# Splitting and joining both 16-bit planes of a DMA transposition in one instruction, for 8 of 24 rows of tokens

## The chip, the cores and the metric

The kernel runs on one core of a Trainium2 chip. The core has five engines that run their own instruction streams in order and wait for each other by semaphores: PE (TensorE, matrix products, writes PSUM), DVE (VectorE), ACT (ScalarE), POOL (GpSimd) and SP (SyncE, which here only issues DMAs). The metric is the device time of one execution in microseconds, as the median of several runs.

## The reference

Chunked attention with memory keys, followed by a two-layer network with a softmax-weighted, normalised hidden layer (cut to the core):

```python
# attention: 4 batches, 8 heads, 768 positions, head_dim 64; chunks of 32 queries
scores = scale * q_c @ k_full.T            # k_full: 8 memory keys + 56 keys of context
a = exp(scores - max(scores)); a = a / (sum(a) + 1e-9)
out_c = a @ v_full
x = out.transpose(0, 2, 1, 3).reshape(3072, 512)
# network, per row of x
h = x @ w_in                               # 512 -> 1024
e = exp(h - max(h)); sm = e / (sum(e) + 1e-9)
solu = h * sm
ln = (solu - mean(solu)) / sqrt(var(solu) + 1e-6) * g_ln
return ln @ w_out                          # 1024 -> 512
```

## The kernel before

The 3072 tokens are 24 **rows of tokens** t of 128 each, and 12 pairs u of such rows (t = 2u and 2u + 1). All work is cut into steps, and the string ORDER at the top of the file lists every step in the order in which it is written to the engines; no scheduler moves anything. A name such as `Us6.1@G` is the step Us of row 6, part 1, on POOL (`@S` ACT, `@G` POOL, `@V` DVE). Since each engine runs in order, the place of a name in ORDER decides what stands in front of an instruction on its engine.

The steps of the attention go by pairs: loads of k, q and v on SP (Lk, Lq, Lv), scores on PE (S), row maximum and its subtraction on DVE (M, Bm), exponentials on ACT (X), row sums on DVE (Z), the transposed probabilities (p), values on PE (V), normalisation on DVE (N), and the transposed result (x). The rounded high part XH of x and the remainder XL (x minus XH, on DVE at L215) are what G reads: `hidden` (L482), four blocks of six matmuls G t.0 to G t.3 for each row, of which the third matmul of a block is the first one that reads XL.

The steps of the network go by rows: G, row maximum Hm (DVE L491), exponential He (ACT L496), product and sum Hu (DVE L506, L509), square Sq (ACT L514), subtraction of the mean C (DVE L524), four small instructions Dn for the scale (POOL L530 to L533), the transposition of u, its high part UH and remainder UL, and O: `project` (PE L543), eight blocks of three matmuls O t.0 to O t.7; then scaling Os and the store St from ACT.

A transposition of a 128x1024 float32 tile (p, x or u) goes through DMA, which transposes 16-bit elements only. Two split instructions copy the lower and the upper halves of all words into two planes of 1024 16-bit elements (Ps, Xs, Us; part 0 and part 1). One DMA transposition issued from SP (Px, Xx, Ux; L338) moves both planes. Two join instructions interleave the planes again (Pm, Xm, Um). A split or a join is one copy of 128x1024 16-bit elements, on ACT (L210) or on POOL (L212); ORDER says which. All tiles of this path lie in 12 buffers "slot" of SBUF, taken and given back in a ring.

The PSUM buffers "two" (three of them) hold, in turn, the scores of a pair, the values of a pair and the hidden row h. A new holder waits until the last reader of the one before is done: h is free after Sq, scores after Bm, values after N.

```python
def halves(ap):
    return ap.bitcast(U16).rearrange("p (n two) -> p two n", two=2)
def planes(ap):
    return ap.bitcast(U16).rearrange("p (two n) -> p two n", two=2)
```

Of the kernel before, what the change touches and what calls it, by code (L numbers as in the profile page):

```python
# [33 lines left out]
W7@S R8 D14 G0.3 D15 W8@S G1.3 Hm0 A10 G2.3 B10 He0 Hm1 R9 A11 E10 H10@S Hu0 He1 B11 T10 H11@S E11
R10 Sq0 Hu1 W9@S G3.0 Dn0@G T11 A12 C0 Sq1 R11 B12 Hm2 A13 Dn1@G G3.1 H12@S E12 B13 A14 UT0 T12
H13@S E13 G3.2 UH0@S B14 T13 A15 G3.3 E14 H14@S C1 W10@S B15 T14 W11@S R12 H15@S E15 UL0@V He2 R13
T15 W12@S UT1 Hu2 W13@S R14 UH1@S Hm3 Sq2 R15 UL1@V W14@S Dn2@G W15@S C2 O0.0 He3 S2 Hu3 O0.1 Lk4
Lq4 O1.0 O0.2 M2 Sq3 O1.1 O0.3 C3 Dn3@G S3 Bm2 O0.4 Lk5 Lq5 M3 X2 O1.2 O0.5 Ps2.0@G O1.3 Z2 S4
Ps2.1@G Bm3 O0.6 Px2 Lk6 Lq6 UT2 M4 X3 O0.7 UH2@S O1.4 Ps3.0@G Z3 UT3 Os0 Ps3.1@G O1.5 Bm4 UH3@S St0
Px3 O1.6 Pm2.0@G UL2@V X4 O1.7 Pm2.1@G Os1 UL3@V S5 Ps4.0@S St1 Z4 V2 Ps4.1@G O2.0 Pm3.0@S Lv4 N2  # L40
Px4 O3.0 O2.1 M5 Pm3.1@G Xs2.0@S O3.1 O2.2 Xs2.1@G Bm5 V3 Xx2 O2.3 X5 N3 Lv5 Pm4.0@G O3.2 Ps5.0@S
O2.4 Z5 Xs3.0@G O3.3 Pm4.1@S O2.5 Ps5.1@G O3.4 Xs3.1@G Px5 V4 Xm2.0@S Xx3 O2.6 N4 Xm2.1@G O3.5 O2.7
Xs4.0@S XH2@G O3.6 S6 Os2 Xs4.1@G XL2@V Pm5.0@S St2 Lv6 O3.7 Xx4 Os3 Pm5.1@G M6 Lk7 Lq7 G4.0 Xm3.0@S
St3 G5.0 Bm6 Xm3.1@G G4.1 X6 XH3@G G5.1 Xm4.0@S Ps6.0@G Z6 G4.2 Ps6.1@G Xm4.1@S XL3@V Px6 G5.2 XH4@G
G4.3 XL4@V G5.3 Hm4 G6.0 Pm6.0@G Hm5 He4 G6.1 Pm6.1@G He5 Hu4 G6.2 Hu5 Sq4 G6.3 Sq5 C4 Dn4@G G7.0
Hm6 Us4.0@S Dn5@G G8.0 C5 He6 Us4.1@G G7.1 Us5.0@S Hu6 Ux4 G8.1 Us5.1@G Sq6 G7.2 Ux5 G8.2 C6 Dn6@G
Lk8 Lq8 Us6.0@S G7.3 Um4.0@G Us6.1@S V5 Hm7 Um4.1@G Ux6 G8.3 Um5.0@S N5 Lv7 UH4@G He7 Hm8 G9.0
Xs5.0@G Um5.1@G UL4@V Xs5.1@S G9.1 He8 UH5@G Xx5 G9.2 Hu7 Um6.0@S O4.0 G9.3 UL5@V Sq7 Um6.1@G O4.1
Hu8 O5.0 Xm5.0@S O4.2 Dn7@G C7 O5.1 UH6@S Hm9 O4.3 Xm5.1@G Us7.0@S O5.2 UL6@V O4.4 XH5@G Sq8 O5.3
O4.5 Us7.1@S C8 O5.4 Dn8@G O4.6 He9 Ux7 XL5@V O5.5 Us8.0@G O4.7 Hu9 G10.0 Os4 Us8.1@G St4 Sq9 O5.6  # L50
V6 Ux8 C9 Dn9@G Um7.0@S O5.7 Lv8 N6 G10.1 Us9.0@G Os5 Xs6.0@S St5 S7 Um7.1@G Us9.1@S Xs6.1@G O6.0 M7
Lk9 Lq9 G10.2 UH7@S Ux9 Um8.0@G Xx6 Bm7 O6.1 Um8.1@G G10.3 UL7@V X7 UH8@G O6.2 Ps7.0@S G11.0 Hm10
Ps7.1@S O6.3 Um9.0@G Z7 O7.0 He10 Px7 O6.4 Um9.1@G UL8@V G11.1 Xm6.0@S O6.5 Xm6.1@G Hu10 O7.1 O6.6
G11.2 Pm7.0@G Sq10 O6.7 Pm7.1@G C10 O7.2 Os6 G11.3 XH6@G UH9@S St6 Us10.0@S O7.3 Hm11 Dn10@G V7
Us10.1@S XL6@V O7.4 He11 Ux10 O8.0 N7 O7.5 G12.0 UL9@V Xs7.0@G O7.6 Lv9 Hu11 G12.1 Xs7.1@G Sq11 O7.7
Um10.0@G Xx7 G12.2 Os7 C11 Dn11@G Um10.1@S St7 S8 Us11.0@G UH10@S O8.1 M8 Lk10 Lq10 G12.3 Us11.1@G
UL10@V Xm7.0@S O8.2 Ux11 G13.0 Bm8 Xm7.1@G O8.3 Hm12 O9.0 X8 O8.4 Ps8.0@G Z8 G13.1 He12 Um11.0@G
O8.5 Ps8.1@S Hu12 O9.1 Um11.1@G Px8 O8.6 Sq12 G13.2 C12 Dn12@G O8.7 O9.2 Os8 G13.3 XH7@G Us12.0@S
St8 UH11@G O9.3 Pm8.0@S XL7@V S9 Us12.1@G Pm8.1@S O9.4 Hm13 Lk11 Lq11 G14.0 Ux12 M9 He13 O9.5 G14.1
UL11@V O9.6 Bm9 O10.0 O9.7 Hu13 X9 Um12.0@G V8 Os9 Z9 Ps9.0@G G14.2 Lv10 Sq13 St9 Um12.1@G N8 O10.1  # L60
Ps9.1@S G14.3 Dn13@G C13 UH12@S Px9 O10.2 Hm14 Xs8.0@G Us13.0@S G15.0 UL12@V Xs8.1@G He14 O10.3
O11.0 Us13.1@S Hu14 O10.4 Xx8 G15.1 Pm9.0@G Ux13 Sq14 O10.5 Pm9.1@G O11.1 C14 O10.6 Dn14@G G15.2
Us14.0@S Xm8.0@G O10.7 Us14.1@S O11.2 Xm8.1@G G15.3 Os10 Ux14 Um13.0@S St10 O11.3 XH8@G Hm15 V9
Um13.1@S XL8@V O11.4 Lv11 He15 UH13@G O12.0 N9 O11.5 Um14.0@S G16.0 UL13@V Xs9.0@G Um14.1@S O11.6
Hu15 G16.1 Xs9.1@G Sq15 O11.7 Xx9 G16.2 UH14@G Os11 C15 Dn15@G St11 S10 UL14@V Us15.0@S O12.1 M10
G16.3 Us15.1@G Xm9.0@G Ux15 Bm10 O12.2 G17.0 Xm9.1@G Hm16 X10 O12.3 Ps10.0@G Z10 O13.0 He16 O12.4
Ps10.1@G G17.1 Hu16 Um15.0@S Px10 O12.5 Sq16 O13.1 Um15.1@G O12.6 G17.2 C16 Dn16@G Us16.0@S S11
Us16.1@G Pm10.0@S O12.7 M11 O13.2 Ux16 XH9@G Os12 G17.3 Pm10.1@S UH15@G Bm11 St12 O13.3 XL9@V X11
V10 Hm17 Ps11.0@G O13.4 G18.0 Um16.0@S Ps11.1@G N10 O13.5 He17 Um16.1@G Px11 UL15@V G18.1 Xs10.0@S
O13.6 O14.0 Xs10.1@G Hu17 O13.7 G18.2 Xx10 Os13 UH16@G Z11 Sq17 St13 Pm11.0@G O14.1 UL16@V G18.3  # L70
Dn17@G Pm11.1@S O14.2 C17 G19.0 Hm18 Us17.0@G Xm10.0@S O14.3 Us17.1@G He18 V11 Xm10.1@G Ux17 O14.4
N11 O15.0 O14.5 Hu18 Xs11.0@G G19.1 Xs11.1@G Sq18 O14.6 O15.1 Xx11 Um17.0@G C18 O14.7 G19.2 Os14
XH10@G Um17.1@S St14 O15.2 Us18.0@G G19.3 XL10@V Dn18@G Us18.1@S O15.3 O16.0 Xm11.0@S Hm19 UH17@G
Ux18 O15.4 G20.0 UL17@V He19 Xm11.1@G O15.5 Hu19 G20.1 O15.6 Sq19 Um18.0@G O16.1 O15.7 C19 Dn19@G
Um18.1@S G20.2 XH11@G Os15 O16.2 Us19.0@S G20.3 St15 UH18@G Us19.1@G G21.0 Hm20 Ux19 O16.3 He20
G21.1 Hu20 O16.4 G21.2 Sq20 O16.5 Um19.0@G O17.0 C20 O16.6 Dn20@G Um19.1@S G21.3 Us20.0@G O16.7
XL11@V UH19@S O17.1 Us20.1@G Os16 O17.2 Hm21 St16 G22.0 Ux20 UL18@V He21 O17.3 G22.1 UL19@V O17.4
Hu21 G22.2 Sq21 O17.5 Um20.0@G G22.3 C21 Dn21@G Um20.1@S O17.6 Hm22 O18.0 Us21.0@G O17.7 He22 O18.1
UH20@G G23.0 Os17 Us21.1@G Hu22 St17 O18.2 Ux21 G23.1 UL20@V Sq22 O18.3 C22 Dn22@G O19.0 Us22.0@S
O18.4 G23.2 Us22.1@G Um21.0@S O18.5 Ux22 O19.1 Um21.1@G O18.6 G23.3 O18.7 Hm23 UH21@G O19.2 Os18  # L80
UL21@V O19.3 He23 Um22.0@G St18 O20.0 O19.4 Hu23 O20.1 O19.5 Um22.1@G Sq23 O20.2 O19.6 UH22@G C23
O20.3 Dn23@G O19.7 UL22@V O20.4 Os19 UT23 St19 O21.0 UH23@S O20.5 O21.1 UL23@V O20.6 O21.2 O20.7
O21.3 Os20 O21.4 St20 O22.0 O21.5 O22.1 O21.6 O22.2 O21.7 O22.3 Os21 O22.4 St21 O23.0 O22.5 O23.1
O22.6 O23.2 O22.7 O23.3 Os22 O23.4 St22 O23.5 O23.6 O23.7 Os23 St23
"""


# [554 lines left out]
```

## Time and profile before

| what | value |
|---|---|
| median of 3 runs | 381.53 us |
| the runs | 376.96, 381.53, 382.13 us |
| the profiled execution: span from its first to its last instruction | 379.2 us (its own time is not listed beside it; the span lies 2.3 us below the median of the runs) |
| PE busy | 354.1 us (93%) |
| DVE, ACT, POOL busy | 220.7, 199.4, 199.5 us (58%, 53%, 53%) |
| mean granted clock of PE | 0.972 |
| DMA transpositions | 39, median 5.2 us from issue to landing |

A row of a timeline has the start in us, the duration in us, engine, line, operation, the tiles written and read with shapes, the number of instructions merged, and in brackets the idle time of the engine ahead of it and what ended that. A row of a group has the count, the busy time, the mean duration in ns, and the idle time ahead of the group with its releasers.

### The profile page before, as it was taken

The numbers are of one execution on the slowest core, as the hardware profiler recorded it, in microseconds if no ns is written. First come the engines' busy times: TensorE is split into PE (matmuls) and PEld (weight loads), VectorE is DVE, ScalarE is ACT, GpSimd is POOL, SyncE is SP. The second block draws the span as 40 slices with busy tenths as digits, with TensorE's granted clock in tenths as the row PEclk, the third lists the DMA queues.
The fourth block names the chain that finished last, engine by engine and source line by source line (L and its number), as shares of the span: only waits on it lengthen the run. The fifth ranks groups of instructions, "written<-read, shape, count | busy, mean of one in ns | idle before, by whom it ended". The sixth has DMA issues, their size and how long they took to land.

```text
span 379.2 us, 10107 instructions
## 1 busy us (share of the span) xinstructions
PE 354.1 (93%) x4408; PEld 279.3 (74%) x4408; DVE 220.7 (58%) x287; ACT 199.4 (53%) x259; POOL 199.5 (53%) x236
## 2 busy tenths in 40 slices
...
GB/s 277 399 404 404 251 114 3 0 143 291 135 259 188 236 162 62 217 183 131 309 159 195 218 114 213 199 201 161 111 127 99 140 56 85 84 74 93 28 55 55
DMA packets 96859, 62.90 MB, mean 166 GB/s; under 512 B 82480, under 2 KB 82480, under 8 KB 96816
## 3 DMA queue, kind: packets, MB, share of 16 engines
...
HBM read 35.52 MB, written 6.29 MB: 110 GB/s over the span
## 4 chain that ended last, share of the span: by engine, by line
PE 69%; DMA 11%; POOL 6%; issue 5%; ACT 5%; DVE 3%; POOLq 0%; ACTq 0%
PE one L543 28%; PE two L482 24%; DMA slot<-slot 11%; PE two L434 4%; POOL slot L212 4%; PE two L372 3%; PE one L286 3%; PE two L357 3%; PE two L199 2%; DVE fr L215 1%; ACT two L514 1%; ACT slot L210 1%; ACT fr L210 1%; PE one L288 1%; PE one L287 1%
## 5 line engine op out<-in xcount | busy, mean ns | idle before, releaser
L212 POOL TENSOR_SCALAR slot<-slot 128x1024 uint16<-128x1024 uint16 x94 | 119.6, 1296 | 61.3 <-DMA slot<-slot 34.1
L482 PE MATMUL two<-w_in_h,fr 128*128 128x512 f32 x384 | 134.0, 401 | 6.9 <-ACT two L514 3.7
L543 PE MATMUL one<-w_out_h,fr 128*128 128x512 f32 x384 | 135.9, 404 | 0.1
L210 ACT COPY slot<-slot 128x1024 uint16<-128x1024 uint16 x62 | 73.3, 1206 | 45.0 <-DMA slot<-slot 30.8
L482 PEld LDWEIGHTS two<-w_in_h,fr 128*128 128x128 f32 x384 | 72.9, 190 | 24.3 <-ACT two L514 4.4
L543 PEld LDWEIGHTS one<-w_out_h,fr 128*128 128x128 f32 x384 | 73.1, 190 | 20.1 <-issue 1.8
L543 PE MATMUL one<-w_out_l,fr 128*128 128x512 f32 x192 | 76.4, 398 | 1.5 <-issue 1.5
L482 PE MATMUL two<-w_in_l,fr 128*128 128x512 f32 x192 | 76.4, 398 | 0.0
L215 DVE TENSOR_TENSOR fr<-slot,fr 128x1024 fp32r<-128x1024 f32 x29 | 43.3, 1497 | 23.1 <-POOL fr L212 18.7
L491 DVE TENSOR_REDUCE per_row<-two 128x1 f32<-128x1024 f32 x24 | 29.1, 1218 | 28.2 <-PE two L482 28.1
L482 PEld LDWEIGHTS two<-w_in_l,fr 128*128 128x128 f32 x192 | 36.6, 191 | 10.1 <-issue 1.9
L543 PEld LDWEIGHTS one<-w_out_l,fr 128*128 128x128 f32 x192 | 36.6, 191 | 7.7
L514 ACT ACTIVATE two<-slot,per_row 128x1024 f32<-128x1024 f32 x24 | 26.8, 1117 | 23.5 <-DVE per_row L509 23.5
L496 ACT ACTIVATE slot<-two,per_row 128x1024 f32<-128x1024 f32 x24 | 26.8, 1116 | 18.0 <-DVE per_row L491 17.1
L212 POOL TENSOR_SCALAR fr<-slot 128x1024 fp32r<-128x1024 f32 x23 | 25.6, 1119 | 18.7 <-ACT slot L210 9.2
L524 DVE TENSOR_SCALAR slot<-slot,per_row 128x1024 f32<-128x1024 f32 x24 | 22.1, 922 | 21.8 <-ACT two L514 21.6
L551 ACT ACTIVATE o_sb<-one,per_row 128x512 f32<-128x512 f32 x24 | 16.4, 684 | 34.5 <-PE one L543 34.5
L506 DVE CUSTOM_DVE_ANT_0 slot<-two,slot 128x1024 f32<-128x1024 f32 x24 | 29.1, 1213 | 5.8 <-ACT slot L496 5.8
L530 POOL TENSOR_SCALAR per_row<-per_row 128x1 f32<-128x1 f32 x24 | 10.9, 453 | 33.0 <-ACT slot L496 31.3
L409 ACT ACTIVATE slot<-slot 128x1024 f32<-128x1024 f32 x12 | 12.7, 1061 | 29.1 <-DVE slot L401 29.1
L446 DVE TENSOR_TENSOR slot<-two,per_head 128x1024 f32<-128x1024 f32 x12 | 14.6, 1217 | 21.7 <-PE two L434 15.0
L434 PE MATMUL two<-v,slot 64*32 64x64 f32 x1536 | 19.6, 239 | 7.1 <-issue 5.5
...
## 6 DMA issues: line engine op xcount, KB each, us to landing
...
slot<-in_w_in SPq DMA_DIRECT2D x8, 512.0 KB, 12.0
...
slot<-slot SPq DMA_TRANSPOSE x39, 5.2
g_col<-in_g_ln SPq DMA_DIRECT2D x1, 4.0 KB, 12.3
```

Of the source, the lines that this page charges most:

```text
L210: nc.scalar.copy(out, in_)
L212: nc.gpsimd.tensor_scalar(out, in_, 1.0, 0.0, ALU.mult, ALU.add)
L215: (nc.gpsimd if on == "G" else nc.vector).tensor_tensor(out, a, b, ALU.subtract)
L434: nc.tensor.matmul(x[32 * j:32 * j + 32, r, t, g], pT[rows, t, g, 32 * j:32 * j + 32], vv[rows, t, g, j], start=True, stop=True,)
L482: nc.tensor.matmul(h[:, half], x[a], w[b][:, c, half * HALF:(half + 1) * HALF], start=c == 0 and i == 0, stop=c == NC_ - 1 and i == 2,)
L491: nc.vector.tensor_reduce(take("per_row", ("hm", t), 1), flat(get("h", t)), axis=AX.X, op=ALU.max, negate=True)
L496: nc.scalar.activation(take("slot", ("u", t), 3), flat(get("h", t)), AF.Exp, bias=get("hm", t), scale=1.0, accum_out=take("per_row", ("esu ...
L506: nc.vector.tensor_tensor_reduce(u, flat(get("h", t)), u, 1.0, 0.0, ALU.mult, ALU.add, accum_out=usum)
L514: nc.scalar.activation(flat(get("h", t)), get("u", t), AF.Square, bias=get("nmu", t), scale=1.0, accum_out=take("per_row", ("var", t), 1),)
L524: nc.vector.tensor_scalar(u, u, get("nmu", t), None, ALU.add)
L543: nc.tensor.matmul(get("o", t), u[a], w[b][:, f], start=f == 0 and i == 0, stop=f == NF - 1 and i == 2)
L551: nc.scalar.mul(take("o_sb", ("osb", t), 1), get("o", t), get("rstd", t))
```

## The change

For rows 6, 7, 8, 9 and 12, 13, 14, 15 of tokens the two splits Us become one instruction and the two joins Um become one instruction, each of 2 x 1024 16-bit elements. The instruction stands in ORDER where the second part stood. The engines are DVE for rows 6, 9, 12 and 15, ACT for rows 7 and 13, POOL for rows 8 and 14; split and join of a row are on one engine. Rows 6, 7, 8 and 12 walk plane by plane (Usb, Umb: first all lower halves, then all upper ones). Rows 9, 13, 14 and 15 walk element by element (Use, Ume: lower and upper half of a word, then the next word). So 32 copies of 1024 elements go (18 on ACT, 14 on POOL), and 16 of 2048 elements come (8 on DVE, 4 on ACT, 4 on POOL). The DMA transpositions and their places on SP stay.

```diff
+    def split_both(name, elements):
+        def step(i, on):
+            s = planes(take("slot", (name + "s", i), 1))
+            x = halves(get(name, i))
+            if elements:
+                s, x = (ap.rearrange("p two n -> p n two") for ap in (s, x))
+            copy(on, s, x)
+            used(name, i)
+            used(name, i)
+        return step
+
+    def join_both(name, uses, elements):
+        def step(i, on):
+            out = halves(take("slot", (name + "T", i), uses))
+            x = planes(get(name + "t", i))
+            if elements:
+                out, x = (ap.rearrange("p two n -> p n two") for ap in (out, x))
+            copy(on, out, x)
+            used(name + "t", i)
+            used(name + "t", i)
+        return step
...
-        UT=on_pe("u"), Us=split("u", 2), Ux=xbar("u"), Um=join("u", 2), UH=high("u", 1), UL=low("u", 1),
+        UT=on_pe("u"), Us=split("u", 2), Ux=xbar("u"), Um=join("u", 2),
+        Usb=split_both("u", False), Use=split_both("u", True),
+        Umb=join_both("u", 2, False), Ume=join_both("u", 2, True), UH=high("u", 1), UL=low("u", 1),
```

In ORDER, for example, `Us12.0@S ... Us12.1@G` becomes `Usb12@V`, and `Us14.0@S Xm8.0@G O10.7 Us14.1@S O11.2 Xm8.1@G` becomes `Xm8.0@G O10.7 Use14@G O11.2 Xm8.1@G`.

Three places show what that does to the streams. The first is DVE around the split of row 12. Before, behind the remainder of pair 7 (fr_74, XL7) stand the row maximum of h13, a memset and the row maximum of the scores of pair 9 (M9), the remainder UL11, and Bm9:

```order
L215 TENSOR_TENSOR fr_74<-slot_65,fr_75 128x1024
L491 TENSOR_REDUCE per_row_114<-two_82 128x1
L389 MEMSET two_83 32x2x4x16
L393 TENSOR_REDUCE per_head_99<-two_83 128x16
L215 TENSOR_TENSOR fr_80<-slot_68,fr_73 128x1024
L401 TENSOR_TENSOR slot_71<-two_83,per_head_99 128x2x8x64
```

Now (line numbers of the changed file; L207 is the copy on DVE) the split of row 12 is in between:

```order
L214 TENSOR_TENSOR fr_74<-slot_63,fr_75 128x1024
L207 COPY slot_69<-slot_72 128x2048
L512 TENSOR_REDUCE per_row_114<-two_82 128x1
L410 MEMSET two_83 32x2x4x16
L414 TENSOR_REDUCE per_head_99<-two_83 128x16
L214 TENSOR_TENSOR fr_80<-slot_68,fr_73 128x1024
L422 TENSOR_TENSOR slot_66<-two_83,per_head_99 128x2x8x64
```

Everything from the row maximum of h13 to Bm9 has moved behind one more copy.

The second place is POOL around the split of row 14. Before, behind the joins Pm9 come the four instructions of Dn14, both joins Xm8 and the high part XH8 (fr_77), then UH13 (fr_75):

```order
L212 TENSOR_SCALAR slot_72<-slot_65 128x1024 x2
L530 TENSOR_SCALAR per_row_109<-per_row_109 128x1
L531 TENSOR_SCALAR per_row_109<-per_row_109 128x1
L532 TENSOR_SCALAR per_row_109<-per_row_104,per_row_109 128x1
L533 TENSOR_TENSOR per_row_123<-per_row_109,mhalf 128x1
L212 TENSOR_SCALAR slot_66<-slot_68 128x1024 x2
L212 TENSOR_SCALAR fr_77<-slot_66 128x1024
L212 TENSOR_SCALAR fr_75<-slot_64 128x1024
```

Now the split of row 14 (128x1024x2), which was on ACT, stands between the two joins Xm8:

```order
L211 TENSOR_SCALAR slot_71<-slot_63 128x1024 x2
L551 TENSOR_SCALAR per_row_109<-per_row_109 128x1
L552 TENSOR_SCALAR per_row_109<-per_row_109 128x1
L553 TENSOR_SCALAR per_row_109<-per_row_104,per_row_109 128x1
L554 TENSOR_TENSOR per_row_123<-per_row_109,mhalf 128x1
L211 TENSOR_SCALAR slot_66<-slot_68 128x1024
L211 TENSOR_SCALAR slot_65<-slot_62 128x1024x2
L211 TENSOR_SCALAR slot_66<-slot_68 128x1024
L211 TENSOR_SCALAR fr_77<-slot_66 128x1024
L211 TENSOR_SCALAR fr_75<-slot_64 128x1024
```

XH8 has moved behind that copy, and so has what reads it.

The third place is ACT around the split of row 13. Before, the two parts stand on both sides of the exponential He14 (L496), and Sq14 (L514) and the two parts of row 14 follow:

```order
L210 CAST fr_76<-slot_69 128x1024
L210 COPY slot_62<-slot_63 128x1024
L496 ACTIVATE slot_61,per_row_109<-two_81,per_row_117 128x1024
L210 COPY slot_62<-slot_63 128x1024
L514 ACTIVATE two_81,per_row_104<-slot_61,per_row_100 128x1024
L210 COPY slot_71<-slot_61 128x1024 x2
```

Now one instruction stands between He14 and Sq14, and those of row 14 are gone:

```order
L209 CAST fr_76<-slot_70 128x1024
L517 ACTIVATE slot_62,per_row_109<-two_81,per_row_117 128x1024
L209 COPY slot_69<-slot_67 128x1024x2
L535 ACTIVATE two_81,per_row_104<-slot_62,per_row_100 128x1024
```

More of the change, by code (lines that the diff above doesn't have):

```diff
@@ L34 @@
[L34 to L84, printed above, removed]
+V0 T0 H0@S B1 A3 R0 Lv2 N0 H1@S W0@S E1 XT0 B3 A2 T1 H3@S B2 R1 XH0@S E3 E2 H2@S T3 W1@S XL0@V R3
```

57 lines of the change are left out of this document (53 added, 4 removed).

## The prediction

> **What bounds the kernel now.** I read the busy times first, then a table by stage, then what PE waits for.
>
> ```profile
> span 379.2 us, 10107 instructions
> PE 354.1 (93%) x4408; PEld 279.3 (74%) x4408; DVE 220.7 (58%) x287; ACT 199.4 (53%) x259; POOL 199.5 (53%) x236
> ```
>
> ```profile
> 140.00:150.00 10.00, 7.03 (x24) 5.61 (x24) 7.45 (x14) 8.10 (x15) 7.63 (x14) 0.83 0.12 23
> 180.00:190.00 10.00, 8.30 (x117) 6.70 (x110) 6.81 (x8) 6.05 (x7) 5.91 (x5) 1.00 1.08 308
> 190.00:228.00 38.00, 37.91 (x527) 30.23 (x526) 21.85 (x27) 21.36 (x25) 26.83 (x30) 1.00 0.83 168
> ```
>
> The columns after the stretch are its length, then busy PE, PEld, DVE, ACT, POOL, the granted clock, DMA share and GB/s. From 190 to 228 us PE stands idle for 0.09 us. The whole list of PE's waits from 143.1 us to the end is short:
>
> ```profile
> PE two L482 <- issue: 1.7, 1, 1.7
> PE two L482 <- DVE fr L215: 0.4, 1, 0.4
> PE two L372 <- issue: 0.3, 1, 0.3
> ```
>
> That is 2.4 us. The changed steps run between 150 and 272 us, so this is all that they could win back, and two of the three waits are put down to nothing on DVE, ACT or POOL. The copies that go belong to engines that are busy for about half of the span. The question is therefore not how much busy time ACT and POOL lose but whether a longer copy, standing in front of something that PE needs soon, opens a gap in PE's stream.
>
> **What the copies cost.** These are the splits and joins as groups, and one split (Us13.0) and one join (Um13.0) on ACT:
>
> ```profile
> L212 POOL TENSOR_SCALAR slot<-slot 128x1024 uint16<-128x1024 uint16 x94 | 119.6, 1296 | 61.3 <-DMA slot<-slot 34.1
> L210 ACT COPY slot<-slot 128x1024 uint16<-128x1024 uint16 x62 | 73.3, 1206 | 45.0 <-DMA slot<-slot 30.8
> ```
>
> ```profile
> 240.11 1.04 ACT L210 COPY slot<-slot 128x1024 uint16<-128x1024 uint16 x1
> 252.40 1.36 ACT L210 COPY slot<-slot 128x1024 uint16<-128x1024 uint16 x1 [2.70 <-DMA slot<-slot]
> ```
>
> Gone: 18 x 1.21 = 21.7 us of ACT and 14 x 1.30 = 18.1 us of POOL. Both are worth nothing by themselves, since PE is the cover. A split writes neighbours, a join writes every other 16-bit place, and costs 1.36 against 1.04 us. Plane by plane, two of a kind in one instruction should cost 2.1 us (split) and 2.7 us (join) on ACT and POOL; nothing is saved but some overhead.
>
> Element by element the split writes alternately into two planes 2 KB apart. No row shows such writes. The lower bound is two splits, 2.1 us; the nearest row, the join, gives 2.7 us. For the upper bound I suppose that a write costs by the group of 16 bytes that it touches, as well as by the element: 1024 elements in 128 groups took 1.04 us, in 256 half-filled groups 1.36 us, so a group costs 0.32/128 = 2.5 ns and an element 0.70 ns; with a group of its own for each of 2048 elements that is 6.6 us. The jump is far longer than the join's, so I take a value above the join, a third of the way to the upper bound: **3.9 us**, and keep 2.1 and 6.6. The same goes for the joins that read in this manner.
>
> The Trainium skill, page "Advanced Engine Details and Errata", section "SBUF Cachelines", has such a rule: SBUF has lines of 16 bytes, at least two accesses must hit a line to hide the access latency, and a different line for each access is penalised. It gives no price, so by it the element order is slower by an amount that only a run shows; it speaks against rows 9, 13, 14 and 15, and the two rows above agree with it only as far as a join costs more than a split.
>
> On DVE no 16-bit copy was run. The nearest rows are one-input instructions between SBUF tiles:
>
> ```profile
> 220.57 0.76 DVE L524 TENSOR_SCALAR slot<-slot,per_row 128x1024 f32<-128x1024 f32 x1 [1.31 <-ACT two L514]
> L263 DVE TENSOR_SCALAR slot<-slot 128x512 uint32<-128x512 uint32 x16 | 6.7, 426 | 0.2
> ```
>
> 512 more elements cost 0.76 - 0.43 = 0.33 us, so 2048 would take 0.76 + 2 x 0.33 = **1.4 us**; at the pace of the instructions that take 1.22 us for 1024 it would be 2.4 us. I take 1.4, from the row that is likest.
>
> **Rows 6 to 9 cost nothing.** Usb6 falls into a hole of DVE that ended with
>
> ```profile
> 154.63 1.22 DVE L491 TENSOR_REDUCE per_row<-two 128x1 f32<-128x1024 f32 x1 [4.67 <-PE two L482]
> 192.79 7.03 POOL L212 TENSOR_SCALAR slot<-slot 128x1024 uint16<-128x1024 uint16 x5 [6.80 <-DMA slot<-slot]
> 189.98 1.16 DVE L215 TENSOR_TENSOR fr<-slot,fr 128x1024 fp32r<-128x1024 f32 x1
> 191.06 1.21 DVE L506 CUSTOM_DVE_ANT_0 slot<-two,slot 128x1024 f32<-128x1024 f32 x1
> 195.59 1.13 ACT L514 ACTIVATE two<-slot,per_row 128x1024 f32<-128x1024 f32 x1
> ```
>
> The tightest of the four is Ume9, now on DVE in front of UL8 (189.98) and Hu10 (191.06). It has to wait for the transposition that ended POOL's 6.80 us of idling at 192.79. Hu10 then starts at 192.8 + 1.4 + 1.1 = 195.3 and ends 1.4 later at 196.7; Sq10, at 195.59 before, comes 1.2 us later, and so does all behind it on DVE up to XL6:
>
> ```profile
> 200.83 1.23 DVE L215 TENSOR_TENSOR fr<-slot,fr 128x1024 fp32r<-128x1024 f32 x1 [0.49 <-POOL fr L212]
> 203.94 0.63 PE L482 MATMUL two<-w_in_h,fr 128*128 128x512 f32 x2
> ```
>
> XL6 ended at 202.06, and the third matmul of G12.0, its first reader, ran at 203.94: 1.9 us of cover, more than the delay (if the copy took 2.4 us, the cover would just be used up). UL8 itself then ends at 195.3, far ahead of O8.0.
>
> **Row 12 opens the first gap.** Here are XL7, Hm13 and Bm9 on DVE, and V8 on PE, which needs the PSUM buffer that Bm9 gives free:
>
> ```profile
> 226.59 2.05 DVE L215 TENSOR_TENSOR fr<-slot,fr 128x1024 fp32r<-128x1024 f32 x1 [5.27 <-POOL fr L212]
> 228.57 1.21 DVE L491 TENSOR_REDUCE per_row<-two 128x1 f32<-128x1024 f32 x1
> 232.34 1.22 DVE L401 TENSOR_TENSOR slot<-two,per_head 128x1024 f32<-128x1024 f32 x1
> 234.04 1.48 PE L434 MATMUL two<-v,slot 64*32 64x64 f32 x128
> ```
>
> DVE works without a gap from 226.59. Usb12 stands behind XL7, so it cannot use the 5.27 us of idling ahead, and Bm9, which ended at 233.56, ends 1.34 us later (1.4 less the overlap of 0.08), at 234.90. V8 had 0.48 us of cover: PE waits **0.9 us**. At 2.4 us for the copy it would wait 1.9.
>
> **Row 14 opens the second.** POOL's joins Pm9 (245.40), Xm8 (249.91) and XH8 (252.62), XL8 on DVE, and the third matmul of G16.0, the first that reads XL8:
>
> ```profile
> 245.40 2.89 POOL L212 TENSOR_SCALAR slot<-slot 128x1024 uint16<-128x1024 uint16 x2 [1.55 <-DMA slot<-slot]
> 249.91 2.63 POOL L212 TENSOR_SCALAR slot<-slot 128x1024 uint16<-128x1024 uint16 x2
> 252.62 1.05 POOL L212 TENSOR_SCALAR fr<-slot 128x1024 fp32r<-128x1024 f32 x1
> 253.71 1.23 DVE L215 TENSOR_TENSOR fr<-slot,fr 128x1024 fp32r<-128x1024 f32 x1 [1.38 <-POOL fr L212]
> 255.88 0.62 PE L482 MATMUL two<-w_in_h,fr 128*128 128x512 f32 x2
> 256.34 0.39 PE L482 MATMUL two<-w_in_l,fr 128*128 128x512 f32 x1
> ```
>
> The load Lv10 on SP, He14 on ACT, and the third instruction of Dn14 on POOL:
>
> ```profile
> 235.56 0.37 SPq L226 DMA_DIRECT2D v<-in_vw  x1
> 241.06 1.11 ACT L496 ACTIVATE slot<-two,per_row 128x1024 f32<-128x1024 f32 x1
> 242.07 0.19 ACT L496 ACTIVATION_READ_ACCUMULATOR slot<-two,per_row 128x1 f32 x1
> 249.03 0.27 POOL L532 TENSOR_SCALAR per_row<-per_row,per_row 128x1 f32<-128x1 f32 x1
> ```
>
> From 245.40 POOL has no gap to the end of XH8 at 253.67, that is 8.27 us. Cover is 255.88 - 254.94 = 0.94 us. Lv10 was issued when V8 ended and gave its buffer back, so it moves 0.9 us, and the transposition Px9 behind it, which ends POOL's wait, moves with it (an estimate; the two share the DMA engines): POOL starts at 246.3. Use14 puts 3.9 us into the chain. On ACT, He14 ends at 242.26 + 2.7 = 245.0, since two copies of row 12 (Usb12 and Umb12, 1.34 us each) now stand ahead of its row maximum on DVE; Use13, also 3.9 us, ends at 248.9, and Sq14, 1.2 us long, at 250.1. The third of Dn14, due at 249.03 + 0.9 = 249.9, waits for it: 0.2 us. XH8 then ends at 246.3 + 8.27 + 3.9 + 0.2 = 258.7, XL8 at 259.9. G16.0's third matmul would come at 255.88 + 0.9 = 256.8: PE waits **3.1 us**. With 2.1 us for Use14 it is 1.1, with 2.7 it is 1.7.
>
> Behind that the other chains have the time that PE lost: Use15 and Ume15 on DVE, even at 2.4 us each, push the chain of pair 10 by less than PE's 4 us, and POOL has lost Us15.1 and Um15.1 (2.6 us by the group's mean). I put no further wait there; a third one of the size of a DVE copy would be covered by the range.
>
> **Sum.** 0.9 + 3.1 = 4.0 us: a span of 379.2 + 4.0 = 383.2 us. The page gives no time of its own beside the span; the median of the runs lies 2.3 us above it, so the time is 385.5 us, slower by 1.0%. A change under 2% is about what a measurement of this kernel cannot tell from none; the runs before alone spread over 377 to 382.
>
> **The rivals.** (1) *Hidden*: PE's gaps do not open, 381.5 us. Against it stands the cover of 0.48 and 0.94 us, less than any copy in the profile; it needs Px9 or XL7 to come earlier, from engines that have work taken off them. 10%.
> (2) *DVE takes one element at a time*, 2.4 us: the wait at V8 is 1.9, the second stays, 386.5 us. 13%. For it: a side of each copy has steps of more than one element. Against: L524's pace.
> (3) *Scattered writes at the upper bound*, ending slower by more than 2%. Place: Use13 on ACT and Use14 on POOL. At 6.6 us each, Use13 ends at 251.6, Sq14 at 252.8, Dn14 at 253.7, the first join Xm8 at 255.1, Use14 at 261.7, XL8 at 265.3; PE waits 8.5 us beside the 0.9. A wait of 3 us was followed by slow matmuls:
>
> ```profile
> 143.04 0.79 PE L482 MATMUL two<-w_in_h,fr 128*128 128x512 f32 x1 [2.97 <-ACT two L514]
> 146.19 0.50 PE L482 MATMUL two<-w_in_l,fr 128*128 128x512 f32 x1
> ```
>
> Seven matmuls between these starts took 3.15 us, in the stage whose granted clock is 0.83; at 0.23 us each, the pace of the two from 255.88 to 256.34, they take 1.6, so 1.5 us more are lost: 381.5 + 9.4 + 1.5 = 392.4 us. It passes 2% (7.6 us) from about 5.3 us a copy on. 17%.
> (4) *It does not shorten anything but frees the queue*: the 1.7 us wait without a cause at 184.6 goes and nothing opens, 379.8 us. 5%.
>
> **How the numbers follow.** The forecast, with Use14 between 2.1 and 5 us, gives 383.5 to 387 and holds 55%; predicted is 385.5. The range of 8 in 10 reaches down to 379 (most of the hidden case is in it) and up to 392 (half of rival 3). Faster by over 2% would need 7.6 us where 2.4 are to be had: 2%. Slower by over 2%: rival 3 and a remainder, 18%. Within 2%: 80%.
>
> **What would show it.** In the profile after, PE should wait for DVE L422 or nothing named at V8, some 0.9 us, and for DVE L214 or POOL at G16.0, some 3 us; the copies L207 on DVE should last 1.3 to 1.5 us plane by plane; POOL's 128x1024x2 should stand between two joins and last clearly over 2.7 us. The prediction is wrong if PE has no new wait after 228 us, or if a gap opens between 150 and 228 us, where I put none.

## The result and the profile after

| | before | after |
|---|---|---|
| median of the runs | 381.83 us (4 runs, 376.96 to 382.48) | 401.40 us (4 runs, 398.24 to 403.37) |
| profiled execution: time, span | 379.2 us span | 402.71 us, 400.9 us span |
| mean granted clock of PE | 0.972 | 0.945 |

The ratio is 1.055, 95% interval 1.050 to 1.061: slower by 5.5%, where 1.0% was forecast. The time lies beyond the range (379 to 392 us). Runs clearly slower than the rest of the same kernel are left out of the ratios and their intervals, medians are of all runs, and here and below a ratio differs by up to 0.8% from the quotient of the medians.

The page's busy times after, as span and engines:

```profile
span 400.9 us, 10087 instructions
...
PE 359.6 (90%) x4408; PEld 282.8 (71%) x4408; DVE 235.8 (59%) x295; ACT 195.0 (49%) x245; POOL 209.3 (52%) x226
```

PE runs the same 4408 matmuls and is busy for 5.5 us longer, so some of them ran slower. DVE, which took over eight copies, and POOL, which has ten instructions fewer, are both busier than before (220.7 and 199.5 us). Now the three largest of PE's waits, from the one ahead of 143 us on (in total, times, longest). The whole list has seven lines and 23.0 us; the same list before has four lines and 5.4 us:

```profile
PE two L503 <- POOL fr L211: 11.6, 1, 11.6
PE two L455 <- issue: 4.4, 2, 3.7
PE two L503 <- ACT two L535: 3.1, 1, 3.1
...
```

The wait of 3.1 us is the one that stood at 143.04 us before. New are 11.6 us for the high part XH8 on POOL (at G16.0), and, within the 4.4, waits of 0.7 us at V8 and of 3.7 at V10. The stages show them, and a slow clock (length, PE, PEld, DVE, ACT, POOL, clock, DMA share, GB/s):

```profile
228.00:256.00 28.00, 27.01 (x358) 21.30 (x356) 18.39 (x23) 18.27 (x14) 11.27 (x14) 1.00 0.72 165
256.00:276.00 20.00, 7.50 (x19) 5.35 (x18) 6.52 (x7) 4.47 (x5) 17.63 (x8) 0.57 0.34 95
276.00:300.00 24.00, 20.35 (x367) 16.19 (x369) 20.74 (x18) 8.98 (x11) 17.42 (x17) 0.99 0.61 111
```

From 256 to 276 us PE gets 19 matmuls done at a mean clock of 0.57. The sum is 0.7 + 11.6 + 3.7 us of new waits and 5.5 us of longer busy time, 21.5 us; the spans differ by 21.7. (The smaller waits changed too, up and down, and nearly cancel.)

The copies as groups (busy time, mean ns; split and join, both orders together):

```profile
L207 DVE COPY slot<-slot 128x2048 uint16<-128x2048 uint16 x8 | 18.7, 2342 | 2.6 <-DMA slot<-slot 2.5
...
L209 ACT COPY slot<-slot 128x2048 uint16<-128x2048 uint16 x4 | 16.2, 4042 | 4.7 <-DMA slot<-slot 4.7
...
L211 POOL TENSOR_SCALAR slot<-slot 128x2048 uint16<-128x2048 uint16 x4 | 15.8, 3942 | 0.0
```

Two copies of 1024 took 2.4 to 2.6 us on these engines, so ACT's four copies would be some 10 us and are 16.2. One instruction makes most of the excess on ACT and one on POOL; on DVE there are two, Use9 with 5.54 us and Use15 with 5.68. Here is Use13 on ACT between He14 (L517) and Sq14 (L535), and then POOL, where Dn14 (its third instruction is L553) is followed by Xm8.0, Use14 and Xm8.1 in one row, and by XH8 and UH13 in the next:

```profile
241.61 1.12 ACT L517 ACTIVATE slot<-two,per_row 128x1024 f32<-128x1024 f32 x1 [1.83 <-DVE per_row L512]
...
242.72 9.60 ACT L209 COPY slot<-slot 128x2048 uint16<-128x2048 uint16 x1
251.81 1.42 ACT L535 ACTIVATE two<-slot,per_row 128x1024 f32<-128x1024 f32 x1
```

```profile
253.53 0.73 POOL L553 TENSOR_SCALAR per_row<-per_row,per_row 128x1 f32<-128x1 f32 x1 [5.19 <-ACT two L535]
...
254.88 11.66 POOL L211 TENSOR_SCALAR slot<-slot 128x1024 uint16<-128x1024 uint16 x3
266.62 2.06 POOL L211 TENSOR_SCALAR fr<-slot 128x1024 fp32r<-128x1024 f32 x2
```

The chain can be read row by row: Use13 takes 9.60 us, Sq14 waits for ACT, POOL idles 5.19 us until Sq14 releases Dn14, and then the three copies take 11.66 us, where the two joins alone took 2.63. G16.0 starts at 267.7. This is the order of events that the third rival of the prediction describes, with a copy nearly half as long again as its worst case.

### The profile page after: what moved, and what is told of

The parts are those of the page before. It is cut to its first block, busy times and chain, and to the rows that moved or that the text cites. A ratio compares the mean times of both kernels' runs of the same rounds, so it can differ in the third digit from the quotient of the medians.

```text
span 400.9 us, 10087 instructions
## 1 busy us (share of the span) xinstructions
PE 359.6 (90%) x4408; PEld 282.8 (71%) x4408; DVE 235.8 (59%) x295; ACT 195.0 (49%) x245; POOL 209.3 (52%) x226
## 5 line engine op out<-in xcount | busy, mean ns | idle before, releaser
L211 POOL TENSOR_SCALAR slot<-slot 128x1024 uint16<-128x1024 uint16 (+1 forms) x84 | 125.7, 1522 | 70.3 <-DMA slot<-slot 38.0
L503 PE MATMUL two<-w_in_h,fr 128*128 128x512 f32 x384 | 135.8, 406 | 19.0 <-POOL fr L211 11.6
L564 PE MATMUL one<-w_out_h,fr 128*128 128x512 f32 x384 | 137.8, 409 | 0.1
L503 PEld LDWEIGHTS two<-w_in_h,fr 128*128 128x128 f32 x384 | 73.9, 193 | 37.8 <-POOL fr L211 12.1
L209 ACT COPY slot<-slot 128x1024 uint16<-128x1024 uint16 (+1 forms) x48 | 68.7, 1454 | 49.5 <-DMA slot<-slot 39.5
L564 PEld LDWEIGHTS one<-w_out_h,fr 128*128 128x128 f32 x384 | 74.4, 194 | 21.3 <-issue 2.4
L564 PE MATMUL one<-w_out_l,fr 128*128 128x512 f32 x192 | 77.5, 404 | 1.9 <-issue 1.9
L214 DVE TENSOR_TENSOR fr<-slot,fr 128x1024 fp32r<-128x1024 f32 x29 | 46.0, 1589 | 37.1 <-POOL fr L211 32.4
L535 ACT ACTIVATE two<-slot,per_row 128x1024 f32<-128x1024 f32 x24 | 27.1, 1130 | 38.1 <-DVE per_row L530 38.1
L517 ACT ACTIVATE slot<-two,per_row 128x1024 f32<-128x1024 f32 x24 | 26.8, 1115 | 20.0 <-DVE per_row L512 15.4
L545 DVE TENSOR_SCALAR slot<-slot,per_row 128x1024 f32<-128x1024 f32 x24 | 19.3, 803 | 23.3 <-ACT two L535 23.2
L455 PEld LDWEIGHTS two<-v,slot 64*32 64x32 f32 x1536 | 17.5, 114 | 14.9 <-issue 10.7
```

The costliest lines, as they stand in the source:

```text
L209: nc.scalar.copy(out, in_)
L211: nc.gpsimd.tensor_scalar(out, in_, 1.0, 0.0, ALU.mult, ALU.add)
L214: (nc.gpsimd if on == "G" else nc.vector).tensor_tensor(out, a, b, ALU.subtract)
L455: nc.tensor.matmul(x[32 * j:32 * j + 32, r, t, g], pT[rows, t, g, 32 * j:32 * j + 32], vv[rows, t, g, j], start=True, stop=True,)
L503: nc.tensor.matmul(h[:, half], x[a], w[b][:, c, half * HALF:(half + 1) * HALF], start=c == 0 and i == 0, stop=c == NC_ - 1 and i == 2,)
L517: nc.scalar.activation(take("slot", ("u", t), 3), flat(get("h", t)), AF.Exp, bias=get("hm", t), scale=1.0, accum_out=take("per_row", ("esu ...
```

## Experiments

Each kernel is compared with runs of the kernel before on the same chip.

**1. All four rows in plane order** (e1_all_by_planes). The changed kernel, with the same instructions at the same places on the same engines, splits in plane order only:

```diff
- Use9@V   Use13@S   Use14@G   Use15@V
+ Usb9@V   Usb13@S   Usb14@G   Usb15@V
```

> The four splits that walked element by element (rows 9, 13, 14, 15) walk plane by plane, on the same engines and at the same places; the joins stay. Theory A (the price of writes that change plane with every element is the loss): DVE, ACT and POOL splits last 1.2, 1.9 and 1.9 to 2.1 us, the 11.6 us gap at G16.0 and the 3.7 us gap at V10 close, the 0.7 us gap at V8 stays, the time is 381.8 + 0.7 = 382.5 us (381 to 384.5). Theory B (the places in the streams make the loss, not the price): a gap at G16.0 stays, 386 us or more.

Measured: 381.77 us, ratio 1.0044 (1.0001 to 1.0087). Groups and waits of PE from 143 us:

```profile
L207 DVE COPY slot<-slot 128x2048 uint16<-128x2048 uint16 x8 | 9.9, 1243 | 3.2 <-DMA slot<-slot 3.2
...
L211 POOL TENSOR_SCALAR slot<-slot 128x2048 uint16<-128x2048 uint16 x4 | 8.5, 2122 | 2.1 <-DMA slot<-slot 2.1
L209 ACT COPY slot<-slot 128x2048 uint16<-128x2048 uint16 x4 | 8.4, 2111 | 0.5 <-ACT o_sb L572 0.5
```

```profile
PE two L503 <- DVE fr L214: 1.8, 2, 1.3
PE two L455 <- issue: 1.5, 2, 0.8
...
```

In place of the waits of 11.6 and 3.7 us there are 1.3 us (for XL8 in G16.0) and 0.8 (V10), and 19.6 us are gone (401.4 against 381.8), all but 0.4% of the 5.5%. The joins of these rows still go element by element. So the order in which four splits write makes the loss. What the rest of the change costs is 0.4%, hardly more than the noise; these two waits and the 0.7 us at V8 are its traces.

**2. and 3. Half of it each** (e2_act_pool_by_planes, e3_dve_by_planes). One kernel puts only rows 13 and 14 (ACT, POOL) back into plane order, the other only rows 9 and 15 (DVE):

```diff
- Use13@S   Use14@G
+ Usb13@S   Usb14@G
```

> Only the splits of rows 13 (ACT) and 14 (POOL) walk plane by plane; those of rows 9 and 15 on DVE stay element by element. Theory A: the G16.0 gap of 11.6 us and the slow matmuls behind it go; Use15 still holds DVE for 5.6 us ahead of Bm10 and POOL with it, so V10 waits 2 to 4 us: 384.5 to 387 us. Theory C (the DVE copies hold POOL back and this makes most of the loss): 395 us or more.

```diff
- Use9@V   Use15@V
+ Usb9@V   Usb15@V
```

> The complement: the splits of rows 9 and 15 (DVE) walk plane by plane, those of rows 13 (ACT) and 14 (POOL) element by element. Theory A: the gap at G16.0 stays at about 11 us with slow matmuls behind it, the gap at V10 goes: 396 to 399 us. Theory C: 385 us or less.

Measured: with ACT and POOL mended 388.18 us, ratio 1.028 (1.017 to 1.038), a little above what was expected; with DVE mended 397.99 us, ratio 1.051 (1.043 to 1.058). The largest waits of PE for each, first with ACT and POOL mended, then with DVE mended:

```profile
PE two L455 <- issue: 5.1, 2, 4.4
PE two L503 <- DVE fr L214: 2.3, 2, 2.1
...
```

```profile
PE two L503 <- POOL fr L211: 11.6, 1, 11.6
...
PE two L455 <- issue: 1.0, 2, 0.7
...
```

The 2.1 us for DVE in the first list stand at 170.03 us, at XL5; in that execution the wait of 3.1 us near 143 us is only 0.4, a trade that experiment 8 meets again. By the ratios the two halves cost 2.8% and 5.1%, together more than the 5.5% of both, but the first interval is wide. The profiled executions add up: their spans lie 3.2 us (383.9) and 16.3 us (397.0) above that of experiment 1 (380.7), and the span of the changed kernel lies 20.2 us above it. The two waits are separate: 11.6 us at G16.0 belong to rows 13 and 14, and the one at V10 (3.7, here 4.4) to the splits on DVE. The profile puts the latter down to "issue"; the rows of DVE and POOL in the changed kernel show where it comes from. L207 is Use15, L422 the Bm10 that V10's probabilities begin with; POOL's row is the join Xm9.0:

```profile
279.34 1.23 DVE L414 TENSOR_REDUCE per_head<-two 128x16 f32<-128x1024 f32 x1 [0.60 <-PE two L393]
280.48 5.68 DVE L207 COPY slot<-slot 128x2048 uint16<-128x2048 uint16 x1
285.72 1.48 DVE L422 TENSOR_TENSOR slot<-two,per_head 128x1024 f32<-128x1024 f32 x1
```

```profile
281.83 5.53 POOL L211 TENSOR_SCALAR slot<-slot 128x1024 uint16<-128x1024 uint16 x1 [1.67 <-DMA slot<-slot]
```

Use15 stands with its 5.68 us between the row maximum M10 and Bm10. And POOL's join Xm9.0 took 5.53 us; in the kernel before it took 1.37 us:

```profile
264.72 1.37 POOL L212 TENSOR_SCALAR slot<-slot 128x1024 uint16<-128x1024 uint16 x1
```

So POOL's copy went on for as long as DVE's ran and ended about 1.2 us behind it. The same shows at Use9 (177.64 to 183.18 us), beside which one POOL copy lasted 6.25 us instead of 1.05. The Trainium skill, page "SBUF — State Buffer", section "Who interferes with whom", names this: a DVE copy that uses two ports holds the port pair that it shares with GpSimd for the whole instruction, and GpSimd is blocked. The two rows agree with it; that these copies use two ports no row shows.

**4. and 5. One chain or two** (e4_act_by_planes, e5_pool_by_planes). Use13 delays POOL through Sq14, and Use14 stands on POOL itself. If both are in one chain, each adds its own length:

```diff
- Use13@S
+ Usb13@S
```

> The changed kernel with only Use13 on ACT put back to plane order (Usb13, about 1.9 us); Use14, Use9 and Use15 stay in element order. Theory A, serial chain: Use13 (9.60 us) ahead of Sq14, Dn14 and the join Xm8.0, and then Use14 (9.25 us) ahead of Xm8.1 and XH8, stand in one chain, so each adds its own length beyond its cover. Without Use13, Dn14 starts near 249.7 us, Xm8.0 ends near 252.4, Use14 near 261.6, XH8 near 264; G16.0 waits 7 to 8.5 us instead of 11.6; time 395 to 400 us, as the wait at V10 of 3.7 us stays. Theory B, one of the two sets the end alone: the wait stays at 11 us or more here and the time at 400 to 403, or it falls below 3 us and the time to 390 or less.

```diff
- Use14@G
+ Usb14@G
```

> The changed kernel with only Use14 on POOL put back to plane order (Usb14, about 1.9 us); Use13, Use9 and Use15 stay in element order. Theory A, serial chain: Use13 holds Sq14 to 252.8 us and Dn14 to 254.4, Xm8.0 ends near 255.7, Usb14 near 257.7, XH8 near 260; G16.0 waits 3.5 to 5 us; time 390 to 396 us. The waits of this run and of the one with Use13 put back then add up to about the 11.6 us. Theory B, one of the two sets the end alone: either the wait stays at 11 us, or it is below 1 us and the time is 387 or less.

Measured: 398.51 us (ratio 1.047, 1.040 to 1.054) and 394.41 us (1.035, 1.029 to 1.041). PE's start of G16.0 in each, with the wait ahead of it:

```profile
260.98 0.80 PE L503 MATMUL two<-w_in_h,fr 128*128 128x512 f32 x1 [7.54 <-POOL fr L211]
```

```profile
259.13 0.80 PE L503 MATMUL two<-w_in_h,fr 128*128 128x512 f32 x1 [4.50 <-POOL fr L211]
```

7.5 + 4.5 = 12.0 us against 11.6 with both: one chain, as expected.

**6. Why an element-order split takes 9.2 to 9.6 us** (m1_strides). Copies by themselves, no network is computed; each copy twice on DVE, ACT and POOL:

```diff
+ for k in (1, 2, 4, 8, 16):
+     on_all(step(d, 1024, k), s[:, 0:1024])
+ for k in (2, 8):
+     on_all(d[:, 0:1024], step(s, 1024, k))
+ on_all(d[:, 0:2048].rearrange("p (two n) -> p n two", two=2), s[:, 0:2048].rearrange("p (n two) -> p n two", two=2))
+ on_all(d[:, 0:2048].rearrange("p (n two) -> p n two", two=2), s[:, 0:2048].rearrange("p (two n) -> p n two", two=2))
+ for g in (2, 8):
+     on_all(planes(d, g), s[:, 0:2048].rearrange("p (n two g) -> p n two g", two=2, g=g))
...
```

> No part of the network is computed: the kernel only copies tiles in SBUF, each pattern twice on DVE, ACT and POOL, one after the other, and stores zeros. Theory L: a write costs 4.6 ns each time that it goes to another group of 16 bytes (from the join with 256 groups, 1.36 us, and Use13 with 2048, 9.60 us). On ACT, 1024 16-bit elements written at a step of 1, 2, 4, 8, 16 elements: 1.04, 1.36, 2.5, 4.9, 4.9 us; alternating planes in runs of 1, 2, 8 elements (2048 elements): 9.6, 4.9, 1.9 us; 512 float32 at a step of 1, 2, 4, 8: 0.6, 1.4, 2.5, 2.5 us; all with contiguous writes about 1.04 (1024) whatever the reads. Theory J (the far jump costs, not the change of group): every fixed step of 2 to 16 about 1.4 us, alternation 9.6. Theory H (going back to the group just left costs): steps up to 16 below 1.5 us, alternation 9.6 us. Theory W (part of a 4-byte word costs a read first): 16-bit steps of 2 to 16 all 1.4 us, float32 at any step 0.6 us.

Rows on ACT, the first of each two (d and s are 16-bit views): 1024 elements written at steps of 1 (behind it a copy of one element), 2, 4, 8 and 16 elements, 1024 read at a step of 8 elements, 2048 written element by element into two planes, the reverse, which reads element by element, and 2048 written into two planes in runs of two elements:

```profile
15.54 1.04 ACT L29 COPY dst<-src 128x1024 uint16<-128x1024 uint16 x1 [13.53 <-DVE src L27]
16.62 0.19 ACT L29 COPY src<-zero 128x1 f32<-128x1 f32 x1
...
23.00 1.33 ACT L29 COPY dst<-src 128x1024 uint16<-128x1024 uint16 x1 [4.89 <-DVE src L27]
...
32.70 2.46 ACT L29 COPY dst<-src 128x1024 uint16<-128x1024 uint16 x1 [6.57 <-DVE src L27]
...
49.18 4.71 ACT L29 COPY dst<-src 128x1024 uint16<-128x1024 uint16 x1 [11.08 <-DVE src L27]
...
74.61 4.46 ACT L29 COPY dst<-src 128x1024 uint16<-128x1024 uint16 x1 [15.53 <-DVE src L27]
...
103.67 1.99 ACT L29 COPY dst<-src 128x1024 uint16<-128x1024 uint16 x1 [5.48 <-DVE src L27]
...
124.07 9.21 ACT L29 COPY dst<-src 128x2048 uint16<-128x2048 uint16 x1 [15.90 <-DVE src L27]
...
165.18 2.12 ACT L29 COPY dst<-src 128x2048 uint16<-128x2048 uint16 x1 [22.23 <-DVE src L27]
...
177.62 1.98 ACT L29 COPY dst<-src 128x2048 uint16<-128x2048 uint16 x1 [7.72 <-DVE src L27]
```

POOL agrees with ACT within 0.03 us; DVE takes 0.43, 0.74, 1.30, 2.43 and about 2.4 us for the steps, and 5.32 for the element-order split. The cost grows with the number of 16-byte groups that are visited, 4.4 ns for each ((4.71 - 2.46) us / 512), and not with the distance of the jump: steps of 16 bytes cost as much as planes 2 KB apart. But runs of two elements, which change the group 1024 times, took only 1.98 us, less than half of the 4.9 that a price by group gave. And reads at a step of 16 bytes took 1.99 us, where theory L had 1.04. None of the theories put down for this run holds as it stands.

**7. Half words or groups** (m2_runs). A rule that fits these rows within 0.06 us, but for the strided reads, of which it says nothing, and the step of 32 bytes (4.70 us by the rule, 4.46 measured), was written down and tried on nine new copies (again alone, no network): 0.19 us for the instruction, and for each visit to a group of 16 bytes the larger of 0.83 ns per element and a floor, 4.4 ns for words written in halves and 1.8 ns for whole ones. The 0.19 us are what a copy of one element took.

```diff
+ for k in (4, 8):
+     for at in (0, 1):      # on a word's border, one element off it
+         on_all(runs(d, 512, 2, k, at), s[:, 0:1024].rearrange("p (n g) -> p n g", g=2))
+ on_all(runs(d, 256, 4, 8, 0), s[:, 0:1024].rearrange("p (n g) -> p n g", g=4))
+ on_all(planes(d, 4), s[:, 0:2048].rearrange("p (n two g) -> p n two g", two=2, g=4))
...
```

> No network is computed: copies by themselves, of 16-bit or 32-bit elements with contiguous reads, each twice on DVE, ACT and POOL. The strides measured so far fit a rule M for ACT and POOL: 0.19 us and, for each visit to a group of 16 bytes, the larger of 0.83 ns per element and a floor, which is 4.4 ns where 32-bit words are written in halves and 1.8 ns where they are written whole. Rival L: the floor is 4.4 ns whatever is written. Rival T: what counts is two hits to a group one after the other, whole word or not. Times on ACT and POOL. Pairs of 16-bit elements (1024 elements) every 8 bytes, on a word's border: M 1.04 us, L 1.32. The same off the border by one element, so that two words are half written: M 1.32, T 1.04. Pairs every 16 bytes, on the border: M 1.10, L 2.44. Off the border: M 2.44, T 1.10. Runs of four elements every 16 bytes (1024): M 1.04, L 1.32. 2048 elements alternating between two planes in runs of four: M and L 1.9 to 2.4. 1024 32-bit elements alternating one by one between two planes: M 2.0, L 4.7. 512 16-bit elements written as 32-bit ones every 16 bytes: M 1.1, L 2.44. 512 32-bit elements written as 16-bit ones every 16 bytes: M and L 2.44, T the same. DVE about half of each, as far as it moves two elements at a time.

Rows on ACT, again the first of each two, in the order of the expectation (the two pairs every 8 bytes, the two every 16 bytes, and so on):

```profile
15.55 1.04 ACT L29 COPY dst<-src 128x1024 uint16<-128x1024 uint16 x1 [13.53 <-DVE src L27]
...
23.01 1.33 ACT L29 COPY dst<-src 128x1024 uint16<-128x1024 uint16 x1 [4.90 <-DVE src L27]
...
31.35 1.10 ACT L29 COPY dst<-src 128x1024 uint16<-128x1024 uint16 x1 [5.21 <-DVE src L27]
...
40.14 2.46 ACT L29 COPY dst<-src 128x1024 uint16<-128x1024 uint16 x1 [6.11 <-DVE src L27]
...
52.61 1.04 ACT L29 COPY dst<-src 128x1024 uint16<-128x1024 uint16 x1 [7.08 <-DVE src L27]
...
59.98 1.90 ACT L29 COPY dst<-src 128x2048 uint16<-128x2048 uint16 x1 [4.81 <-DVE src L27]
...
71.53 1.96 ACT L29 COPY dst<-src 128x1024 f32<-128x1024 f32 x1 [7.28 <-DVE src L27]
...
82.41 1.09 ACT L29 CAST dst<-src 128x512 f32<-128x512 uint16 x1 [6.47 <-DVE src L27]
...
91.15 2.45 ACT L29 CAST dst<-src 128x512 uint16<-128x512 f32 x1 [6.09 <-DVE src L27]
```

All nine agree within 0.04 us with the times put down for rule M. The third and the fourth row differ only in that a pair of elements lies on a word's border or one element off it, in the same group: 1.10 against 2.46 us. So half-written words cost 4.4 ns a group, and an element-order split, which writes 2048 half words in 2048 visits, costs 0.19 + 2048 x 4.4 ns = 9.2 us. Why the hardware takes longer for half words was not measured.

**8. A wait that was there before** (b1_max_first). The 3.0 us that PE waits ahead of G7.0 come from an order on DVE: Hm4 stands behind XL4, which waits for XH4. One move in the kernel before:

```diff
- G4.3 XL4@V G5.3 Hm4 G6.0 Pm6.0@G Hm5 He4
+ G4.3 Hm4 G5.3 Hm5 XL4@V He4 G6.0 Pm6.0@G
```

> The kernel before, with one move: on DVE the row maxima Hm4 and Hm5 stand ahead of XL4 and not behind it. G4.3 ended at 133.1 us, yet Hm4 starts at 137.7, because XL4 waits for XH4 (135.5 to 136.6). Theory: He4 then ends near 136.7, Hu4 near 139.2, Sq4 near 140.5, and the 3.0 us that PE waits for Sq4 ahead of G7.0 fall to 1 us or less; the slow matmuls behind it go too. 2.5 to 4 us less: ratio 0.989 to 0.994. Rival: the time is given back at a later chain, or PE waits for something else at the same place: ratio 0.998 to 1.002.

Measured: 382.58 us against 380.57, ratio 1.009 (1.006 to 1.012): a miss, though the medians of all runs differ by 0.5% only. (The profiled execution, 378.98 us, was the fastest of its runs, so its rows tell where waits are, and not the median.) The wait at G7.0 fell to 1.0 us as expected, and a new one of 3.0 us for XL5 stands at G10.0:

```profile
PE two L482 <- DVE fr L215: 3.4, 2, 3.0
...
PE two L482 <- ACT two L514: 1.0, 1, 1.0
```

The time won was given back 30 us later. Why the kernel became slower, and not only no faster, this execution does not show: its span is 2.1 us shorter than that of the kernel before. Xx5, which XL5 rests on, was issued on SP right behind the load Lv7; its issue lasted 5.27 us and ended at 162.3 us, about when that load landed (162.5).

**9. The load behind the transposition** (b2_load_behind). On top of experiment 8:

```diff
- N5 Lv7 UH4@G ... Xx5 G9.2
+ N5 UH4@G ... Xx5 Lv7 G9.2
```

> The kernel of b1_max_first with one more move, on SP: the load Lv7 stands behind the transposition Xx5 instead of ahead of it. In b1_max_first the 3.0 us won ahead of G7.0 (157 us) are waited for again at G10.0 (167 to 170 us), where PE waits for XL5. There Xx5 was issued at 156.9 us, right behind Lv7, and its issue ended only at 162.2, when Lv7 had landed; Xs5.1 had ended at 154.0. Theory: with Lv7 behind it, Xx5 lands near 158.5 to 160 us instead of 164, the wait at G10.0 falls from 3.0 us to 1 us or less, and what was won ahead of G7.0 stays: ratio to the kernel before 0.985 to 0.995. Rival: another wait of the same size comes in behind it (SP's queue, or the row sums of pair 7): ratio 0.998 to 1.01.

Measured: 376.70 us against 380.75, ratio 0.991 (0.988 to 0.994). The time is as the theory expected. Xx5's issue now lasts 1.95 us and ends at 159.3. (The wait ahead of G7.0, which the expectation puts at 157 us, stands at 138.3 us in experiment 8.) Waits for G7.0 and G10.0 are no longer in the list, which has one of 2.8 us at V7 and one of 0.2. The wait at V7 was 0.4 us in experiment 8, so a new wait did come in, as the rival said, but it did not cost the gain.

**10. and 11. The change as the runs suggest it** (c2_change_mended, d1_row14_in_parts). All splits in plane order, all joins in element order (two cheap forms), Usb12 ahead of XL7, and the moves of experiment 9; then the same with row 14 alone back in two parts on ACT:

```diff
- Use9 Use13 Use14 Use15   Umb6 Umb7 Umb8 Umb12   XL7@V S9 Usb12@V
+ Usb9 Usb13 Usb14 Usb15   Ume6 Ume7 Ume8 Ume12   Usb12@V XL7@V S9
```

> The change as it can be done by what the runs showed: all eight splits plane by plane, all eight joins element by element, each on its engine of the changed kernel; Usb12 on DVE ahead of XL7 and not behind it; and the two moves of b2_load_behind (the row maxima Hm4 and Hm5 ahead of XL4, Lv7 behind Xx5). Theory: splits take 1.2 us on DVE and 1.9 on ACT and POOL, joins 1.2 and 2.1; PE waits neither at V8 nor at G16.0; the time is that of b2_load_behind within 0.5%: ratio 0.985 to 0.997. Rival: a copy in one piece holds a chain at a new place where two pieces on two engines did not, as the 2.1 us ahead of XH8: ratio 1.000 to 1.010.

```diff
- Xm8.0@G ... Usb14@G ... Xm8.1@G      Ume14@G
+ Xm8.0@G ... Us14.0@S Us14.1@S ... Xm8.1@G      Um14.0@S Um14.1@S
```

> The kernel of c2_change_mended with row 14 alone back in two parts on ACT (Us14.0, Us14.1, Um14.0, Um14.1), so that POOL has no copy of row 14 between the joins Xm8.0 and Xm8.1. In c2_change_mended PE waited 0.45 us for XH8 and 1.36 us for XL8 ahead of and in G16.0, with Usb14 (1.9 us) in that chain; its time is 0.8% above b2_load_behind. Theory: the copy in the chain is the cause; the wait at G16.0 falls from 1.8 us to 0.3 us or less, the time by 1 to 2 us: ratio to the kernel before 0.993 to 0.997. Rival: the rest of the 0.8% lies elsewhere (V7, the slow matmuls, the copies on DVE that meet POOL's): the wait goes and the ratio stays at 0.997 to 1.002.

Measured: 380.59 us against 380.75, ratio 0.999 (0.996 to 1.002), above the theory's range, and 375.39 us against 381.06, ratio 0.986 (0.983 to 0.989; 4 runs), below it. The first kernel's waits for POOL's XH8 and DVE's XL8 around G16.0 (rows of PE), and the second kernel's whole list from 120 us on:

```profile
249.59 0.50 PE L503 MATMUL two<-w_in_h,fr 128*128 128x512 f32 x1 [0.45 <-POOL fr L211]
...
251.67 0.50 PE L503 MATMUL two<-w_in_h,fr 128*128 128x512 f32 x1 [1.36 <-DVE fr L214]
```

```profile
PE two L455 <- POOL slot L211: 2.0, 1, 2.0
PE two L503 <- DVE fr L214: 1.0, 1, 1.0
PE two L503 <- ACT two L535: 0.9, 1, 0.9
```

Neither wait at G16.0 is left, and by the ratios the time fell by 1.3%, more than the 1 to 2 us expected. The rows show less: 1.8 us at G16.0 and 0.9 us at V10 (275.88 us in the first kernel) are gone, and the spans of the two profiled executions differ by 2.6 us. The first kernel's profiled execution was 2.8 us faster than its median, so where the rest lies is not located. Even in its cheap form the copy of row 14 between two joins on POOL costs (its join left POOL with it). The second kernel is faster than both kernels of this case. Whether it is faster than that of experiment 9 (0.991), which merges no copies, the runs do not settle, since the intervals meet; so it stays open whether merging brings anything.

## Why the prediction was wrong

**The step that failed is the price of an element-order split**, "3.9 us", with bounds of 2.1 and 6.6. Measured were 9.60 us on ACT, 9.25 on POOL, 5.5 to 5.7 on DVE (taken there as 1.4 or at most 2.4). Even the upper bound was too low, and the reason lies in its working: it let a group's price and an element's price add up and gave the instruction no fixed cost, so that two rows, 1.04 and 1.36 us, fixed both. Experiments 6 and 7 show a fixed 0.19 us and the larger of the two prices. With these the same join row gives (1.36 - 0.19) / 256 = 4.6 ns per group, and 2048 groups 9.6 us. The sum is the larger fault: with the 0.19 us taken out and the two prices still added, the bound would be some 6.4 us (an estimate from the same two rows). The range went with the bound. (A third of the way from 2.7 to 6.6 us is 4.0 and not 3.9, which changes nothing.) The Trainium skill's page "Advanced Engine Details and Errata", section "SBUF Cachelines", cited there, had the direction. Its count of two hits to a line does not decide here: pairs off a word's border hit each group twice and take 2.46 us.

With 9.60 and 9.25 us in the prediction's own chain, PE would wait some 14.2 us at G16.0 (an estimate: rival 3's 8.5, and 3.0 and 2.65 more for the two copies). Measured are 11.6 us for XH8 and 0.9 more for XL8. So the path was right. Most of the difference is that He14 ended 0.6 us later than before and not 2.7 (242.82 against 242.26 us).

**Wrong with it:** "I put no further wait there" behind G16.0. With 5.68 us, Use15 stands ahead of Bm10 for longer than the cover, and V10 waits 3.7 us. The estimate of pair 10's chain used 2.4 us a copy, and the effect of DVE's copy on POOL was not in it. Lv10 was said to delay the joins Pm9 to 246.3 us; they began at 245.0, earlier than before. The slow clock behind a long wait was in rival 3 with 1.5 us, read off a wait of 3 us; behind 11.6 us, and with a second wait at V10, PE's busy time grew by 5.5.

**Right:** that PE bounds the kernel and saved copies bring nothing; that the gap opens at G16.0 through Use13, Sq14, Dn14 and Use14 (the mechanism of rival 3, given 17%); the wait at V8, 0.9 us forecast and 0.7 measured; plane-order copies of 1.2 to 1.3 us on DVE (1.4 forecast) and of 1.9 and 2.5 us on ACT and POOL (2.1 and 2.7); and, nearly, that rows 6 to 9 cost nothing. Between 150 and 228 us, where the prediction put no gap and called one a sign of being wrong, two small ones are in the trace: 0.7 us at 179.4 us (0.3 in the list before) and 0.7 at V7 (199.9 us; none before). In experiment 1 they are 0.4 and 0.8 us, so the order of the writes does not make them, and Use9 with 5.54 us stayed covered.

The joins, which "read in this manner", were forecast like the splits and were not: 2.13 us, cheaper than in plane order. With plane-order splits everywhere (experiment 1) the other terms can be seen by themselves: 0.7 us at V8 for 0.9, and 1.3 us at G16.0 where the prediction has 1.1 for a Use14 of 2.1 us. That this kernel's 381.8 us is close to rival 1's 381.5 is luck: rival 1 has no gaps, and there are three.
